# Polysketch attention and an exact-GELU MLP: keys of batches 1 to 3 by sketches as the stationary operand, numerators next to the query sketches

## The chip, the cores and the metric

The kernel runs on one core of one Trainium2 chip. The metric is the device time of one execution, in microseconds. The kernel before took 267.11 us, the median of three runs (266.31 to 267.64). Its profiled execution spans 264.9 us from the first to the last instruction, with a granted TensorE clock of 1.000.

## The reference

A polynomial-sketch attention (batch B = 4, H = 4 heads, S = 1088 tokens, head size D = 32, sketch size R = 8) feeds an MLP (128 to 2048 to 128, exact GELU) on 4352 tokens. Everything is float32 on the chip.

```python
def phi(x):                                   # 8 + 8 sketches, 64 features per token and head
    a = np.einsum('rd,bhsd->bhsr', S1, x)
    b = np.einsum('rd,bhsd->bhsr', S2, x)
    return np.einsum('bhsi,bhsj->bhsij', a, b).reshape(*x.shape[:-1], r * r)
q_p, k_p = (phi(q), phi(k))
kv = np.einsum('bhsf,bhsd->bhfd', k_p, v)     # sums over the tokens of a batch
z = np.sum(k_p, axis=2)
num = np.einsum('bhsf,bhfd->bhsd', q_p, kv)
den = np.einsum('bhsf,bhf->bhs', q_p, z)[..., None] + 1e-06
attn = num / den
...
h = x @ w_in                                  # x: attn as (B*S, H*D)
g = 0.5 * h * (1.0 + erf(h * inv_sqrt2))
return g @ w_out
```

Of a batch, 1024 tokens are handled in two chunks of 512; the last 64 tokens of all four batches make a ninth chunk of 256.

## The kernel before, in words

**Steps.** The MLP is the long part. A chunk n has 16 steps (fi = 0 to 15), one for each 128 columns of the hidden layer. In a step `hidden` (L691) lets TensorE make one hidden product of xT[n] and w_in into one of two PSUM tiles `h_ps` (bufs=2, L697, in two halves of 64 columns), and ScalarE applies the GELU (L704) into a `block` of four steps. Two steps later or more, `two_products` (L769) multiplies blocks with w_out (L782). It is a seven-product scheme in which GpSimd first adds halves of a block (`token_sums`, L739, four operations a block), and `drain` (L787) takes the two accumulators `o_ps` apart: three ScalarE copies (L794 to L796), six VectorE additions (L798 to L803). `combine` and `store` (L812, L835) finish a chunk and send it out. Chunks 0 and 1 are handled half in this way, half directly.

**Attention between the steps.** The rest is put in at fixed steps, by `at(t, f)` into `slots`. For chunk n, t = (n - 1) * 16 is the first step of chunk n - 1:

- `query_turn` at t - 6: VectorE turns the queries (L535).
- `query_sketch` at t: eight matmuls with S_abc[b] as the stationary operand in tiles of 64x32, 256 columns each (L584). S_abc[b] holds the sketches S1 and S2 and a factor that depends on the batch's z.
- `query_outer` at t: some fifteen VectorE operations turn the sketches in PSUM (L596), make the denominator and the outer products and turn these (L619).
- `attend` at t + 7: eight matmuls of features and kz[b], the numerators (L633, also 64x32 tiles of 256 columns), and a ScalarE copy into xT[n] (L637).

**Keys of batches 1 to 3.** `load_turned_k` brings the keys of a head in four transfers, so that `key_turn_blocks` can turn them 32x32-wise on VectorE (L353). `features_of_all` (at step 16 for batch 1, t + 6 for batch 2, t + 5 for batch 3) multiplies the turned keys kT, as the stationary operand in 64x64 tiles, with the sketches S12: 32 matmuls of 32 columns each (`key_products`, L368), and lets ScalarE copy half of the sketches from PSUM (L954). `outer_of_all` makes the features k_p in four VectorE products (L964), and `add_tokens` adds half and half over the tokens, down to a quarter for k_s (L413, L416; by GpSimd for batch 1, by VectorE else). `add_last` (L418) finishes k_s for batches 2 and 3 with the remainder tokens. `kv_sum` (L449, in `finish_keys`, at step 21 for batch 1, at t + 14 else) sums k_p with v on TensorE, and k_s with `ones` (L446), and `turn_kv` one step later turns the result into kz[b] and, over `sketch_of_z`, into S_abc[b].

**What sets the order.** Each engine works through its own queue. The kernel's last lines tie each instruction to the one before it on its engine, so that the order on an engine is the order of the text: in a step the drain comes first, then the hidden product and its GELU, the token sums, the slots, the store, the products of earlier blocks. PSUM is full: two banks `h_ps`, two `o_ps`, and four in two tiles `w_ps` that keys, sketches, numerators and kv sums take in turn.

Of the kernel before, what the change touches and what calls it, by code (L numbers as in the profile page):

```python
# [16 lines left out]
def kernel(  # L17
# [21 lines left out]
    F = R * R  # L39
# [27 lines left out]
    def work_banks():  # L67

        return wps.tile([128, 2, CW], FP, name="w_ps")
# [4 lines left out]
    def halves(banks):  # L74
        return [banks[:, i] for i in range(2)]
# [23 lines left out]
    def load_main(eng, n, b, heads=slice(0, H)):  # L99
        eng.dma_start(out=main[n, b][:, heads],  # L100
                      in_=src_of[n][b, heads, 0:MAIN, :].rearrange("h (p j) d -> p h j d", j=J))

    def load_turned_k(b):

        src = k[b, :, 0:MAIN, :].rearrange("h (jj t pb jc) d -> h pb t jj (jc d)", jj=4, t=32, pb=4)
        for h in range(H):
            for pb in range(4):
                sp.dma_start(out=main["k", b][pb * 32:(pb + 1) * 32, h].rearrange("t (jj jc) d -> t jj (jc d)", jj=4),
                             in_=src[h, pb])

    def load_q(n):
        at = n % NCH * CW
# [85 lines left out]
    def load_rest():  # L198

        load_w_out(1, gated=True)  # L200
        for i in range(2, len(pieces)):
            load_w_in(i)
            load_w_out(i)
        for b in range(1, B):
            load_turned_k(b)
            load_main(sp, "v", b)
# [19 lines left out]
    kz_first = big.tile([128, 128], FP, name="kz_first")  # L226

    ones = big.tile([128, D], FP, name="ones")

    ones_rem = big.tile([128, D], FP, name="ones_rem")  # L230
    pool.memset(ones_rem, 0.0)
    pool.memset(ones_rem[:REM], 1.0)
# [116 lines left out]
    def key_turn_blocks(b, r):  # L349

        kT[r] = att.tile([128, CW], FP, name="kT")
        for i in range(2):
            dve.transpose(out=kT[r][:, i * 256:(i + 1) * 256].rearrange("p (jc jj t) -> p jj jc t", jc=2, jj=4),  # L353
                          in_=main["k", b][:, r + 2 * i].rearrange("p (jj jc) d -> p jj jc d", jj=4))

    def spread(out, a, b):

        n = a.shape[1]
        return dict(out=out, in0=a[:, :, :, None].broadcast_to([128, n, R, R]),
                    in1=b[:, :, None, :].broadcast_to([128, n, R, R]))  # L360

    def key_products(r, banks, col=0):

        for i in range(2 * NCH):
            for c in range(2):
                for t in range(2):
                    at = i * 128 + c * 64
                    pe.matmul(banks[t][c * 64:(c + 1) * 64, col + i * 32:col + (i + 1) * 32],  # L368
                              lhsT=kT[r][t * 64:(t + 1) * 64, at:at + 64],
                              rhs=S12[t * 64:(t + 1) * 64, 2 * t:2 * t + 2].rearrange("p h r -> p (h r)"),  # L370
                              start=True, stop=True)
# [33 lines left out]

    k_s = {}

    def add_tokens(b, r, eng):

        words = mlp.tile([128, LC], U32, name="bits_r")  # L410
        k_s[r] = words.bitcast(FP).rearrange("p (c two one f) -> p c two one f", c=NP, two=2, one=2)
        kp = k_p[b, r].rearrange("p t (c two one) i j -> p t c two one (i j)", c=NP, two=2)
        eng.tensor_add(out=k_s[r].rearrange("p c two one f -> p (c two one f)"),  # L413
                       in0=kp[:, 0].rearrange("p c two one f -> p (c two one f)"),
                       in1=kp[:, 1].rearrange("p c two one f -> p (c two one f)"))
        eng.tensor_add(out=k_s[r][:, :, 0], in0=k_s[r][:, :, 0], in1=k_s[r][:, :, 1])  # L416

    def add_last(b, eng):  # L418

        rows = slice(b // 2 * REM, (b // 2 + 1) * REM)  # L420
        for r in range(2):
            to = k_s[r][:, :, 0, 0]
            eng.tensor_add(out=to, in0=to, in1=k_s[r][:, :, 0, 1])
            eng.tensor_add(out=to[rows], in0=to[rows], in1=k_p_rem[b % 2][rows, r::2].rearrange("p c i j -> p c (i j)"))

    def flat(features):
        return features.rearrange("p i j -> p (i j)")

# [15 lines left out]
    def kv_product(ps, lhsT, features, h, part, start=False, stop=False):  # L444

        pe.matmul(ps[h * D:(h + 1) * D, part * F:(part + 1) * F], lhsT=lhsT, rhs=features, start=start, stop=stop,  # L446
                  skip_group_check=True)

    def kv_sum(b, ps):  # L449


        for i in range(J):
            ch, t, one = i % 2, i // 4, i // 2 % 2
            for h in range(H):
                kv_product(ps, main["v", b][:, h, i, :], flat(k_p[b, h % 2][:, t, h // 2 * 4 + ch * 2 + one]), h, 0,
                           start=i == 0)
        for h in range(H):
            kv_product(ps, v_rem_aug[b][:, h, :], flat(k_p_rem[b % 2][:, h]), h, 0, stop=True)
        if b == 1:
            for h in range(H):  # L460
                kv_product(ps, ones_rem, flat(k_p_rem[b][:, h]), h, 1)
        for m in range(2 if b == 1 else 1):
            for h in range(H):
                kv_product(ps, ones, k_s[h % 2][:, h // 2, 0, m], h, 1, stop=b > 1 or m == 1)

    kv_T = {}

# [9 lines left out]
        sketch_of_z(b, banks[:, 0], F)  # L477


    S_abc = [big.tile([128, 2, 2, 2 * R], FP, name=f"S_abc{b}") for b in range(B)]  # L480
    own_r = big.tile([128, 2], FP, name="own_r")

    def spread_sketches():

        pool.tensor_add(out=own_r, in0=mask4[:, 0:2], in1=mask4[:, 2:4])
        own = own_r[:, None, :, None]
        w = S_abc[0]
        pool.memset(w, 0.0)
        pool.tensor_mul(out=w[:, :, :, 0:4], in0=sT[:, 0:R].rearrange("p (i f) -> p i f", i=2)[:, :, None].broadcast_to([128, 2, 2, 4]),
                        in1=own.broadcast_to([128, 2, 2, 4]))  # L490
        pool.tensor_mul(out=w[:, :, :, R:], in0=sT[:, None, None, R:].broadcast_to([128, 2, 2, R]),
                        in1=own.broadcast_to([128, 2, 2, R]))
        for b in range(1, B):
            pool.tensor_copy(out=S_abc[b], in_=w)

# [445 lines left out]


    def features_of_all(b):
        banks = halves(work_banks())
        for r in range(2):
            key_products(r, banks, r * 128)
        held["keys"] = banks


        held["factors"] = []  # L950
        for r in range(2):
            a = att.tile([128, 2, J, 2 * R], FP, name="a_t")
            for t in range(2):
                act.copy(out=a[:, t, :, 0:R], in_=factors(banks[t], r)[:, :, 0:R])  # L954
            held["factors"].append(a)

    def factors(bank, r):
        return bank[:, r * 128:(r + 1) * 128].rearrange("p (n r) -> p n r", r=2 * R)

    def outer_of_all(b, adds_by=dve):  # L960
        for r, a in enumerate(held["factors"]):
            k_p[b, r] = att.tile([128, 2, J, R, R], FP, name="k_p")
            for t in range(2):
                dve.tensor_mul(**spread(k_p[b, r][:, t], a[:, t, :, 0:R], factors(held["keys"][t], r)[:, :, R:2 * R]))  # L964
        for r in range(2):
            add_tokens(b, r, adds_by)

    held = {}

# [26 lines left out]
    round_at(14, w_out_sb[4], pool)  # L996
    at(15, query_turn, 2)
    at(16, features_of_all, 1)
    at(16, outer_of_all, 1, pool)
    at(16, turn_keys_rem, 1)  # L1000
    at(17, features_rem, 1)
    at(18, channel_sums, 4)

    at(21, finish_keys, 1)
    at(22, lambda: turn_kv(1, held["kv"]))
    at(23, query_turn, 3)
    at(23, query_sketch, 2)
    at(23, query_outer, 2)
    at(29, attend, 2)
    for i, t in enumerate((25, 26, 28)):  # L1010
        at(t, channel_sums, i)
    at(11, spread_sketches)
# [2 lines left out]
    for n in range(3, NCHUNK):  # L1015

        t = (n - 1) * NF
        b = (n + 1) // 2
        keys = n % 2 and b < B
        if n > 3:  # L1020
            at(t - 6, query_turn, n)
        at(t, query_sketch, n)
        at(t, query_outer, n)
        if keys:
            for r in range(2):
                at(t - 2, key_turn_blocks, b, r)

        at(t + 7, attend, n)
        if keys:
            at(t + 5 + (n == NCH + 1), features_of_all, b)  # L1030
            at(t + 5 + (n == NCH + 1), outer_of_all, b)
            at(t + 6, add_last, b, dve)
            at(t + 8, widen_v_rem, b)
            at(t + 14, finish_keys, b)
            at(t + 15, lambda b=b: turn_kv(b, held["kv"]))


    products = {t: [] for t in range(len(steps) + LAG)}
# [114 lines left out]
```

## Time and profile before

| Engine | busy us | share of the span | instructions |
|---|---|---|---|
| TensorE, matmuls | 258.7 | 98% | 2489 |
| TensorE, weight loads | 133.4 | 50% | 2489 |
| GpSimd | 170.2 | 64% | 180 |
| VectorE | 146.7 | 55% | 315 |
| ScalarE | 118.0 | 45% | 239 |

A float32 matmul stands as two records in the trace, and the end of a matmul is modelled, so that the distance from one start to the next says more than a duration. The costliest group by far is the hidden products (L697), 138.6 us; the products with w_out (L782) come in several groups by operand. The groups that the change touches are small: key products of batches 1 to 3 (L368 into `w_ps`) 3.4 us in 192 records, query sketches (L584) 4.0 and 0.5 us, numerators (L633) 4.0 and 0.7 us, the kv sums of batches 1 to 3 (L446) 5.5 us. On VectorE L964 takes 7.4 us, the additions over tokens (L413, L416, L423, L424) 13.3 us; on GpSimd L413 and L416 take 3.9 us.

The profile tells of each group how long the engine stood idle before it and what ended that. For an engine that isn't the bound such idle time costs nothing by itself; it matters where another engine waits for what comes after.

### The profile page before, as it was taken

The page shows a single profiled execution, that of the slowest core. Times are in us where ns is not written, and L with a number is a line of the kernel's source. Part 1 is how long each engine was busy: PE and PEld are TensorE (multiplying, and loading weights), DVE is VectorE, ACT ScalarE, POOL GpSimd, SP SyncE. Part 2 cuts the span into 40 slices and gives each one's busy share as a digit, 9 for nine tenths or more (in the row PEclk, how much of TensorE's full clock was granted, in tenths as well). Part 3 has the DMA queues.
Part 4 walks back from the last instruction along what each step waited for, and adds up shares of the span by engine and source line. Part 5 has one row for each costly group of instructions (what it writes and reads, how often), then busy time and mean ns, then how long its engine had stood idle before and what let it go on. Part 6 is the DMA issues. An engine that isn't in the chain of part 4 may idle for free.

```text
span 264.9 us, 6135 instructions
## 1 busy us (share of the span) xinstructions
PE 258.7 (98%) x2489; PEld 133.4 (50%) x2489; DVE 146.7 (55%) x315; ACT 118.0 (45%) x239; POOL 170.2 (64%) x180
## 2 busy tenths in 40 slices
PE   8999999999999999999999999999999999999995
PEld 6745445344444545444444554444444444445794
DVE  2985878455499995882086974670276015600240
ACT  5574767523634533353335333533345333533441
POOL 3613007899996876686767786686768677867300
PEclk9999999999999999999999999999999999999999
DMA  6479263433400201102000002002000200020021
GB/s 202 133 223 345 62 177 65 132 89 77 147 13 4 32 10 17 25 2 40 0 2 2 1 7 37 0 2 41 0 0 11 33 2 0 2 40 0 2 36 24
DMA packets 35755, 13.50 MB, mean 51 GB/s; under 512 B 28432, under 2 KB 34320, under 8 KB 35728
## 3 DMA queue, kind: packets, MB, share of 16 engines
q1 hardware_dynamic: 35536, 13.05, 19.5%
q8 instruction: 19, 0.31, 0.5%
q10 hardware_dynamic: 192, 0.07, 0.1%
q14 instruction: 8, 0.07, 0.1%
HBM read 10.88 MB, written 2.23 MB: 49 GB/s over the span
## 4 chain that ended last, share of the span: by engine, by line
PE 93%; DVE 2%; DMA 2%; ACT 1%; issue 1%; SPq 0%; POOL 0%; DVEq 0%
PE h_ps L697 43%; PE o_ps L782 33%; PE o_ps L833 5%; PE w_ps L830 3%; DMA q<-in_q_dram 2%; PE w_ps L584 2%; PE w_ps L633 1%; PE w_ps L446 1%; PE w_ps L368 1%; ACT block L704 1%; PE o_ps L435 0%; PE h_ps L712 0%; PE w_ps L550 0%; PE w_ps L649 0%; DVE x_tok L670 0%
## 5 line engine op out<-in xcount | busy, mean ns | idle before, releaser
L697 PE MATMUL h_ps<-xT,w_in 128*64 128x512 f32 (+3 forms) x516 | 138.6, 576 | 0.0
L704 ACT ACTIVATE block<-h_ps 128x512 f32<-128x512 f32 (+1 forms) x128 | 73.1, 571 | 120.3 <-PE h_ps L697 120.2
L782 PE MATMUL o_ps<-block,w_out 128*64 128x256 f32 x224 | 58.2, 382 | 0.0
L697 PEld LDWEIGHTS h_ps<-xT,w_in 128*64 128x64 f32 (+1 forms) x516 | 42.4, 143 | 28.8 <-issue 10.6
L747 POOL TENSOR_TENSOR bits_low<-block 128x512 f32<-128x512 f32 x28 | 36.0, 1286 | 25.5 <-ACT block L704 25.5
L782 PEld LDWEIGHTS o_ps<-block,w_out 128*64 128x64 f32 x224 | 29.4, 137 | 35.5 <-issue 24.2
L748 POOL TENSOR_TENSOR bits_a<-block 128x512 f32<-128x512 f32 x28 | 35.8, 1277 | 14.7 <-ACT block L704 14.7
L749 POOL TENSOR_TENSOR bits_e<-bits_a,block 128x512 f32<-128x512 f32 x28 | 36.3, 1297 | 2.2
L750 POOL TENSOR_TENSOR bits_m<-block,bits_e 128x512 f32<-128x512 f32 x28 | 36.0, 1284 | 2.2
L782 PE MATMUL o_ps<-bits_a,small 128*64 128x256 f32 x112 | 29.2, 383 | 0.0
L782 PE MATMUL o_ps<-bits_low,small 128*64 128x256 f32 x112 | 29.0, 382 | 0.0
L782 PE MATMUL o_ps<-bits_m,w_out 128*64 128x256 f32 x112 | 29.0, 382 | 0.0
L782 PE MATMUL o_ps<-block,small 128*64 128x256 f32 x112 | 29.0, 382 | 0.0
L596 DVE STREAM_TRANSPOSE w_ps<-w_ps 128x512 f32<-128x512 f32 (+1 forms) x7 | 4.8, 686 | 40.8 <-PE w_ps L584 40.7
L798 DVE TENSOR_TENSOR sums<-o_ps,sums 64x512 f32<-64x512 f32 x8 | 5.5, 683 | 37.6 <-ACT sums L795 26.4
L782 PEld LDWEIGHTS o_ps<-block,small 128*64 128x64 f32 x112 | 14.8, 137 | 19.8 <-issue 11.3
L782 PE MATMUL o_ps<-bits_e,small 128*64 128x256 f32 x112 | 16.8, 379 | 0.0
L833 PE MATMUL o_ps<-g,w_out 128*128 128x512 f32 x32 | 16.4, 599 | 0.1
L782 PEld LDWEIGHTS o_ps<-bits_m,w_out 128*64 128x64 f32 x112 | 14.8, 137 | 0.0
L782 PEld LDWEIGHTS o_ps<-bits_low,small 128*64 128x64 f32 x112 | 14.8, 137 | 0.0
L782 PEld LDWEIGHTS o_ps<-bits_a,small 128*64 128x64 f32 x112 | 14.6, 137 | 0.0
L782 PEld LDWEIGHTS o_ps<-bits_e,small 128*64 128x64 f32 x112 | 8.0, 137 | 11.0 <-issue 9.4
(186 smaller groups left out, 304.7 us busy)
## 6 DMA issues: line engine op xcount, KB each, us to landing
block<-in_moe_w_in_dram SPq DMA_DIRECT2D x3, 512.0 KB, 7.8
block<-in_moe_w_out_dram SPq DMA_DIRECT2D x3, 512.0 KB, 11.5
k<-in_k_dram SPq DMA_DIRECT2D x48, 32.0 KB, 1.8
v<-in_v_dram SPq DMA_DIRECT2D x3, 512.0 KB, 4.3
q<-in_q_dram SPq DMA_DIRECT2D x24, 64.0 KB, 3.4
out_dram<-oT SPq DMA_DIRECT2D x24, 64.0 KB, 2.2
k<-in_k_dram SPq DMA_DIRECT2D x2, 256.0 KB, 2.8
q<-in_q_dram SPq DMA_DIRECT2D x2, 256.0 KB, 4.1
```

The source lines that it names most:

```text
L584: pe.matmul(ps[q4 * 32:(q4 + 1) * 32, c, i * N:(i + 1) * N], lhsT=S_abc[batch_of(n, s, i)][rows, fh].rearrange("p r x -> p (r x)"), rhs=qT ...
L596: dve.transpose(out=tok, in_=ps[:, :, :H2])
L697: pe.matmul(ps[rows, :W], lhsT=w[:, rows], rhs=xT[n][:, :W], start=True, stop=True)
L704: act.activation(out=g_of[n, fi][:, :W], in_=ps[:, :W], func=ACT.Gelu)
L747: pool.tensor_sub(out=s[3], in0=a11, in1=a21)
L748: pool.tensor_add(out=s[1], in0=a21, in1=a22)
L749: pool.tensor_sub(out=s[2], in0=s[1], in1=a11)
L750: pool.tensor_sub(out=s[4], in0=a12, in1=s[2])
L782: pe.matmul(acc[n][bank][half * 64:(half + 1) * 64, col:col + HW], lhsT=fixed, rhs=moving, start=opens and e == 0 and name in "4715", stop ...
L798: dve.tensor_add(out=C[lo, 1], in0=a1[lo], in1=C[lo, 0])
L830: pe.matmul(o_of[n][i][:, :128], lhsT=g[:, i * 128:(i + 1) * 128], rhs=w_tile(w_out_sb, fi), start=first, stop=final)
L833: pe.matmul(o_of[n], lhsT=w_tile(w_out_sb, fi), rhs=g, start=first, stop=final)
```

## The change

Keys of batches 1 to 3 are now handled as the queries are. They are loaded by four transfers a batch, a quarter of the partitions for each head, and turned in two VectorE operations. The sketches S_ab become the stationary operand (eight matmuls of 64x32 tiles and 256 columns in place of 32 of 32 columns), the result is turned in PSUM, and the features come from two VectorE products of 1024 elements. The sum over tokens is then two reductions on VectorE, from k_p into PSUM, for all batches; of the 128 partitions of the sum one half is copied into k_s by ScalarE, the other gets the remainder tokens added by VectorE on the way. The values are loaded in the order that belongs to it. Fewer TensorE instructions, less work in additions and one way for all batches are what it is for.

Beside this, the numerators of chunk n - 1 and the sketches of chunk n now stand directly one after the other, one step before chunk n - 1 begins. They have the same tile shape.

```diff
-    def load_turned_k(b):
+    def load_keys(b):
...
         for h in range(H):
-            for pb in range(4):
-                sp.dma_start(out=main["k", b][pb * 32:(pb + 1) * 32, h].rearrange("t (jj jc) d -> t jj (jc d)", jj=4),
-                             in_=src[h, pb])
+            sp.dma_start(out=main["k", b][h * 32:(h + 1) * 32].rearrange("t x j d -> t (x j d)"),
+                         in_=k[b, h, 0:MAIN, :].rearrange("(t n) d -> t (n d)", t=32))
...
     def features_of_all(b):
-        banks = halves(work_banks())
-        for r in range(2):
-            key_products(r, banks, r * 128)
-        held["keys"] = banks
...
-                act.copy(out=a[:, t, :, 0:R], in_=factors(banks[t], r)[:, :, 0:R])
...
+        ps = work_banks()
+        for g in range(4):
+            for c in range(NP):
+                rows = slice(c * 64, (c + 1) * 64)
+                pe.matmul(ps[g * 32:(g + 1) * 32, c, :CW // 2], lhsT=S_ab[rows].rearrange("p r x -> p (r x)"),
+                          rhs=kT[g // 2][rows, g % 2 * 256:(g % 2 + 1) * 256], start=True, stop=True)
+        held["keys"] = ps
...
+    def outer_of_all(b):
...
+        dve.transpose(out=tok, in_=ps[:, :, :CW // 2])
...
+        dve.tensor_copy(out=a, in_=x[:, :, :, 0:R])
...
+            dve.tensor_mul(out=features.rearrange("p n r (i j) -> p (n r) i j", i=R),
+                           in0=a[:, c, :, :, None].broadcast_to([128, 2 * J, R, R]),
+                           in1=x[:, c, :, None, R:].broadcast_to([128, 2 * J, R, R]))
...
+    def add_tokens(b):
+
+        sums = held["keys"][:, :, :2 * F]
+        for c in range(NP):
+            dve.tensor_reduce(out=sums[:, c], in_=k_p[b][c].rearrange("p n r f -> p (r f) n"), axis=mybir.AxisListType.X,
+                              op=AX.add)
+        k_s[b] = att.tile([128, H, F], FP, name="k_s", bufs=1)
+        to = k_s[b].rearrange("p (c r) f -> p c (r f)", c=NP)
+        rows, rest = (slice(x * REM, (x + 1) * REM) for x in (b // 2, 1 - b // 2))
+        act.copy(out=to[rest], in_=sums[rest])
+        dve.tensor_add(out=to[rows], in0=sums[rows], in1=k_p_rem[b % 2][rows].rearrange("p (c r) i j -> p c (r i j)", c=NP))
...
     at(16, features_of_all, 1)
-    at(16, outer_of_all, 1, pool)
+    at(16, outer_of_all, 1)
     at(16, turn_keys_rem, 1)
     at(17, features_rem, 1)
+    at(17, add_tokens, 1)
...
-        at(t, query_sketch, n)
-        at(t, query_outer, n)
+        at(t - 1, attend, n - 1)
+        at(t - 1, query_sketch, n)
+        at(t - 1, query_outer, n)
...
-        at(t + 7, attend, n)
+        if n == NMAIN:
+            at(t + 15, attend, n)
         if keys:
             at(t + 5 + (n == NCH + 1), features_of_all, b)
             at(t + 5 + (n == NCH + 1), outer_of_all, b)
-            at(t + 6, add_last, b, dve)
+            at(t + 5 + (n == NCH + 1), add_tokens, b)
             at(t + 8, widen_v_rem, b)
-            at(t + 14, finish_keys, b)
-            at(t + 15, lambda b=b: turn_kv(b, held["kv"]))
+            at(t + 13, finish_keys, b)
+            at(t + 14, lambda b=b: turn_kv(b, held["kv"]))
```

Not shown: the values are loaded in four transfers a batch; `kv_sum` takes k_s[b] for all batches in four matmuls, and `ones_rem` and its matmuls for batch 1 are gone; S_ab is made by GpSimd in `spread_sketches`.

More of the change, by code (lines that the diff above doesn't have):

```diff
@@ L101, in load_main, with load_values @@
                       in_=src_of[n][b, heads, 0:MAIN, :].rearrange("h (p j) d -> p h j d", j=J))
-    def load_turned_k(b):
-        src = k[b, :, 0:MAIN, :].rearrange("h (jj t pb jc) d -> h pb t jj (jc d)", jj=4, t=32, pb=4)
+    def load_keys(b):
         for h in range(H):
-            for pb in range(4):
-                sp.dma_start(out=main["k", b][pb * 32:(pb + 1) * 32, h].rearrange("t (jj jc) d -> t jj (jc d)", jj=4),
-                             in_=src[h, pb])
+            sp.dma_start(out=main["k", b][h * 32:(h + 1) * 32].rearrange("t x j d -> t (x j d)"),
+                         in_=k[b, h, 0:MAIN, :].rearrange("(t n) d -> t (n d)", t=32))
+    def load_values(b):
+        src = v[b, :, 0:MAIN, :].rearrange("h (t q n) d -> q t h (n d)", t=32, q=4)
+        for g in range(4):
+            sp.dma_start(out=main["v", b][g * 32:(g + 1) * 32].rearrange("t h n d -> t h (n d)"), in_=src[g])
     def load_q(n):
@@ L204, in load_rest @@
         for b in range(1, B):
-            load_turned_k(b)
-            load_main(sp, "v", b)
+            load_keys(b)
+            load_values(b)
             for c in range(NCH):
@@ L228 @@
     ones = big.tile([128, D], FP, name="ones")
-    ones_rem = big.tile([128, D], FP, name="ones_rem")
-    pool.memset(ones_rem, 0.0)
-    pool.memset(ones_rem[:REM], 1.0)
     v_rem_aug = [big.tile([128, H, D if b else 2 * D], FP, name=f"v_rem_aug{b}") for b in range(B)]
@@ L347, in key_turn, with key_turn_blocks @@
         kT[r] = transposed(ps, "kT", [four_tokens("k", b, h, c) for h in (r, r + 2) for c in range(NCH)], copy, midway)
[L349 to L354, printed above, removed]
+    def key_turn_blocks(b, x):
+        kT[x] = att.tile([128, CW], FP, name="kT")
+        dve.transpose(out=kT[x], in_=main["k", b][:, 2 * x:2 * x + 2].rearrange("p x j d -> p (x j d)"))
     def spread(out, a, b):
@@ L406 @@
     k_s = {}
[L408 to L420, printed above, removed]
-        for r in range(2):
-            to = k_s[r][:, :, 0, 0]
-            eng.tensor_add(out=to, in0=to, in1=k_s[r][:, :, 0, 1])
-            eng.tensor_add(out=to[rows], in0=to[rows], in1=k_p_rem[b % 2][rows, r::2].rearrange("p c i j -> p c (i j)"))
     def flat(features):
@@ L452, in kv_sum @@
         for i in range(J):
-            ch, t, one = i % 2, i // 4, i // 2 % 2
             for h in range(H):
-                kv_product(ps, main["v", b][:, h, i, :], flat(k_p[b, h % 2][:, t, h // 2 * 4 + ch * 2 + one]), h, 0,
-                           start=i == 0)
+                kv_product(ps, main["v", b][:, h, i, :], k_p[b][h // 2][:, i, h % 2], h, 0, start=i == 0)
         for h in range(H):
             kv_product(ps, v_rem_aug[b][:, h, :], flat(k_p_rem[b % 2][:, h]), h, 0, stop=True)
[L459 to L464, printed above, removed]
+        for h in range(H):
+            kv_product(ps, ones, k_s[b][:, h], h, 1, stop=True)
     kv_T = {}
@@ L477, in turn_kv @@
         sketch_of_z(b, banks[:, 0], F)
+    S_ab = big.tile([128, 2, 2 * R], FP, name="S_ab")
     S_abc = [big.tile([128, 2, 2, 2 * R], FP, name=f"S_abc{b}") for b in range(B)]
@@ L492, in spread_sketches @@
                         in1=own.broadcast_to([128, 2, 2, R]))
+        pool.tensor_mul(out=S_ab, in0=sT[:, None].broadcast_to([128, 2, 2 * R]), in1=own_r[:, :, None].broadcast_to([128, 2, 2 * R]))
         for b in range(1, B):
@@ L943, in features_of_all @@
     def features_of_all(b):
-        banks = halves(work_banks())
-        for r in range(2):
-            key_products(r, banks, r * 128)
-        held["keys"] = banks
[L950 to L953, printed above, removed]
-                act.copy(out=a[:, t, :, 0:R], in_=factors(banks[t], r)[:, :, 0:R])
-            held["factors"].append(a)
-    def factors(bank, r):
-        return bank[:, r * 128:(r + 1) * 128].rearrange("p (n r) -> p n r", r=2 * R)
@@ L960, in outer_of_all @@
[L960 to L966, printed above, removed]
+        ps = work_banks()
+        for g in range(4):
+            for c in range(NP):
+                rows = slice(c * 64, (c + 1) * 64)
+                pe.matmul(ps[g * 32:(g + 1) * 32, c, :CW // 2], lhsT=S_ab[rows].rearrange("p r x -> p (r x)"),
+                          rhs=kT[g // 2][rows, g % 2 * 256:(g % 2 + 1) * 256], start=True, stop=True)
@@ new lines, in features_of_all @@
+        held["keys"] = ps
+    def outer_of_all(b):
+        ps = held["keys"]
+        tok = ps[:, :, CW // 2:]
+        dve.transpose(out=tok, in_=ps[:, :, :CW // 2])
+        x = tok.rearrange("p c (k x) -> p c k x", x=2 * R)
+        a = att.tile([128, NP, 2 * J, R], FP, name="a_t")
+        dve.tensor_copy(out=a, in_=x[:, :, :, 0:R])
+        k_p[b] = []
+        for c in range(NP):
+            features = att.tile([128, J, 2, F], FP, name="k_p")
+            dve.tensor_mul(out=features.rearrange("p n r (i j) -> p (n r) i j", i=R),
+                           in0=a[:, c, :, :, None].broadcast_to([128, 2 * J, R, R]),
+                           in1=x[:, c, :, None, R:].broadcast_to([128, 2 * J, R, R]))
+            k_p[b].append(features)
@@ new lines, in add_tokens @@
+    def add_tokens(b):
+        sums = held["keys"][:, :, :2 * F]
+        for c in range(NP):
+            dve.tensor_reduce(out=sums[:, c], in_=k_p[b][c].rearrange("p n r f -> p (r f) n"), axis=mybir.AxisListType.X,
[5 more added lines that the diff above has]
+        dve.tensor_add(out=to[rows], in0=sums[rows], in1=k_p_rem[b % 2][rows].rearrange("p (c r) i j -> p c (r i j)", c=NP))
@@ L1006 @@
     at(23, query_turn, 3)
-    at(23, query_sketch, 2)
-    at(23, query_outer, 2)
-    at(29, attend, 2)
+    at(24, query_sketch, 2)
+    at(24, query_outer, 2)
     for i, t in enumerate((25, 26, 28)):
```

## The prediction

> **What bounds the kernel now.** First the busy table and the chain of waits on the page:
>
> ```profile
> PE 258.7 (98%) x2489; PEld 133.4 (50%) x2489; DVE 146.7 (55%) x315; ACT 118.0 (45%) x239; POOL 170.2 (64%) x180
> ...
> PE 93%; DVE 2%; DMA 2%; ACT 1%; issue 1%; SPq 0%; POOL 0%; DVEq 0%
> ```
>
> TensorE is the bound: 98% busy and 93% of the chain. So a microsecond off its queue is a microsecond off the time, and so is a microsecond of waiting put into it. Second, who TensorE waits for after the start-up:
>
> ```profile
> PE w_ps L864 <- PEq L1137: 0.8, 1, 0.8
> PE w_ps L584 <- DVE S_abc L502: 0.7, 2, 0.6
> ```
>
> Only 0.7 us in two waits, both of a query sketch for its S_abc. Everything else arrives in time, and the question is how much in time. Third, TensorE's timeline at the keys of batch 3:
>
> ```profile
> 139.98 1.03 PE L697 MATMUL h_ps<-xT,w_in 128*64 128x512 f32 x4
> 140.94 1.14 PE L368 MATMUL w_ps<-S,kT 64*64 64x32 f32 x64
> 142.00 1.08 PE L697 MATMUL h_ps<-xT,w_in 128*64 128x512 f32 x4
> 142.91 0.38 PE L782 MATMUL o_ps<-block,small 128*64 128x256 f32 x1
> ...
> 144.21 1.03 PE L697 MATMUL h_ps<-xT,w_in 128*64 128x512 f32 x4
> 145.17 0.66 PE L633 MATMUL w_ps<-q_pT,kz 64*32 64x256 f32 x16
> 145.76 0.43 PE L782 MATMUL o_ps<-block,w_out 128*64 128x256 f32 x1
> ```
>
> Read the starts, since ends overlap. A hidden product (L697) takes 0.86 us, a pair of products (L782) 0.215. The key products take 1.06 plus 0.10 and 0.05 at their borders, 1.21 in all. The numerators (L633: 64x32 tiles, 256 columns) take 0.59 plus the same 0.15, so 0.74. Fourth, ScalarE at the drain before batch 2:
>
> ```profile
> 82.80 0.58 ACT L794 COPY sums<-o_ps 64x512 f32<-64x512 f32 x1
> 85.23 0.37 ACT L795 COPY sums<-o_ps 64x256 f32<-64x256 f32 x1 [1.85 <-DVE oT L845]
> 85.62 0.37 ACT L796 COPY sums<-o_ps 64x256 f32<-64x256 f32 x1
> 85.89 0.59 ACT L704 ACTIVATE block<-h_ps 128x512 f32<-128x512 f32 x1
> ```
>
> One copy waits 1.85 us for VectorE, and the GELU behind it runs only at 85.89 although its hidden product started at 82.72. That was hidden by the two h_ps buffers. Fifth, VectorE at batch 3, with the rows that price the new work:
>
> ```profile
> 141.05 0.68 DVE L798 TENSOR_TENSOR sums<-o_ps,sums 64x512 f32<-64x512 f32 x1 [1.84 <-PE h_ps L697]
> ...
> 143.62 0.42 DVE L803 TENSOR_TENSOR sums<-o_ps,sums 64x256 f32<-64x256 f32 x1
> 143.96 2.46 DVE L964 TENSOR_TENSOR k_p<-a_t,w_ps 128x512 f32<-128x512 f32 x4
> ```
>
> ```profile
> L616 DVE TENSOR_TENSOR q_f<-q_ac,w_ps 128x512 f32<-128x512 f32 x12 | 7.7, 684 | 0.2
> L413 DVE TENSOR_TENSOR bits_r<-k_p 128x512 f32<-128x512 f32 x4 | 5.4, 1343 | 0.0
> L596 DVE STREAM_TRANSPOSE w_ps<-w_ps 128x512 f32<-128x512 f32 x6 | 4.3, 723 | 26.6 <-PE w_ps L584 26.5
> L605 DVE TENSOR_REDUCE w_ps<-q_ac 128x32 f32<-128x128 f32 x6 | 1.8, 295 | 0.2
> ```
>
> **What the Trainium skill says.** "TensorE: Matmul & The Clock Gate", the table at its head: the queues of ScalarE and VectorE are strict FIFO. The trace agrees (the GELU at 85.89). The same page, "What's actually happening": TensorE falls to half clock after an idle window of about 3.4 us. The trace shows only the start: the first six matmuls (L864, 128x256) came 0.47 us apart, those of that size later 0.215. "Advanced Engine Details and Errata", "SBUF Cachelines": one access per 16-byte line costs a penalty, without a figure; no row here reads SBUF so. "SBUF — State Buffer", "Who interferes with whom": two SBUF inputs contend with GpSimd and a reduction doesn't; L413 with 1343 ns against L616 with 684 agrees on the first.
>
> **The change part by part.** *Keys.* 32 key products become 8 of the numerators' shape: 1.21 to 0.74 us, three times: -1.4. *Numerators next to sketches.* Six times two blocks of 0.74 become one with one set of borders and 0.43 us more (1024 cycles at the rate of L697): 1.17 instead of 1.48: -1.9. The hidden product that follows waits for xT: the GELU ahead (0.60) and the copy (0.59) end some 1.5 us after the last hidden product has been issued, and numerators, sketch and two products fill just that: 0. *Batch 1's kv sum* loses 16 of its records: -0.25. *Sketches after a batch change* now have products and a hidden product between turn_kv and themselves: the 0.7 us wait goes. *Loads, S_ab and GpSimd's lost additions* (3.9 us) lie beside TensorE: 0. Sum of what TensorE gains: -4.3.
>
> *The token sums.* Before, VectorE or GpSimd made all of k_s, and only the kv sum some eight steps later waited. Now act.copy in add_tokens moves one half of k_s, and stands in ScalarE's queue right behind the key step's GELU. It waits for VectorE: the drain, then transpose 0.73, copy 0.42 (as L679), two outer products of 1024 elements at 1.22 (L616's slope), two reductions of 1024. The reductions: L605 (128 elements, 295 ns) and L501 (64, 228 ns) give 1.05 ns an element, so 1.23 us; if the line penalty doubles the slope, 2.3. I take the middle, 1.75 each. Behind the copy stands the next GELU, which frees the h_ps buffer that the second hidden product after it needs, and TensorE runs in order. On the clock of before:
>
> - Batch 3: drain ends 144.04; transpose, copy and products to 147.75; reductions to 151.3; act.copy (0.37) to 151.7; GELU to 152.35; hidden product at 152.4. TensorE, from 139.98: hidden 0.96, sketches 0.6, hidden 0.9, three pairs of pairs 1.28, hidden 0.87, products 0.86: there at 145.45. It stalls 6.95.
> - Batch 2: VectorE has no idle time from the drain at 69.94 to that at 88.63, so TensorE gains nothing in there: it now arrives at the opening products at 85.6 and waits until 86.4 for L798 (+0.8, +0.1 for the second bank). Then 88.63 + 3.7 + 3.5 + 0.4 + 0.65 = 97.0 against 89.55: 7.4. Together 8.3.
> - Batch 1: no drain, but VectorE is rounding weights until 45.93. Then 3.65 for transpose to products, 0.41 for k_p_rem, 3.5 for the reductions, 0.45 and 0.65: GELU done at 54.75. TensorE has two more steps here and arrives at 49.82: 5.0.
>
> Sum of stalls +20.2. Stalls of 5 to 7 us may also cost the clock: at the page's window two or three of them would, each the half of some 2.8 us of slow running that the start shows, 1.4; I take 2.0 for all, between 0 and 4.2. Sum: 267.1 - 4.3 + 20.2 + 2.0 = **285.0**.
>
> **The rivals.** *TensorE's gain stands* (4%): if the copy doesn't hold the GELUs, 267.1 - 4.3 = 262.8, faster. For it: VectorE is idle 45% of the span. Against: it is busy just there (drain ahead, 3.65 us of outer products), and even with reductions for nothing batch 3's GELU would end at 148.9, 3.4 us late. *Short stalls* (6%): half the stalls hidden by an order or early readiness that I misread: 267.1 - 4.3 + 10 = 273. *Ends low* (20%): reductions at 1.23 and no clock loss: stalls 17.1, so 279.9. *Ends high* (20%): reductions at 2.3 and three cold starts: stalls 23.5 + 4.2, so 290.5. *VectorE as the bound throughout* speaks against itself: its sum falls, since L413, L416, L423 and L424 (13.3 us) give way to 6 reductions and small adds. The likeliest, 285.0, has 50%.
>
> **How the numbers follow.** From 279 to 291 takes in both ends of the reductions and of the clock, and leaves out the two rivals below (10%) and a little above. Faster by over 0.5%: 4% (the first rival). Within 0.5%: 1%, taken from the short stalls. Slower: 95%.
>
> **What would show it.** Right: ScalarE's longest waits are a 64x256 copy into k_s, for VectorE's reduction, three times, and TensorE has three gaps of 4 to 8 us at hidden products that wait for the GELU. Key sketches take about 0.6 us. The reduction's mean, near 1.2 or near 2.3 us, tells the penalty; matmuls at 0.43 us instead of 0.215 after a gap tell the clock. Wrong: gaps under 1 us there, or TensorE waiting for DMA or xT.

## The result and the profile after

| | before | after |
|---|---|---|
| time, median of 4 runs each, us | 267.16 (266.31 to 267.64) | 290.94 (290.1 to 292.11) |
| ratio to before, 95% interval | 1 | 1.0897 (1.0847 to 1.0947) |
| profiled span, us | 264.9 | 288.7 |
| mean granted TensorE clock | 1.000 | 0.963 |

The change costs 23.8 us. The forecast was 285.0, with 279 to 291 as the range. The direction and the mechanism were right; the time lies at the very end of the range, and one term of the sum, the slow clock, was far too small. The busy table and the chain of the page after, against those of before:

```profile
PE 264.1 (91%) x2329; PEld 133.8 (46%) x2329; DVE 150.7 (52%) x302; ACT 117.4 (41%) x230; POOL 165.4 (57%) x175
...
PE 68%; DVE 16%; SPq 6%; DMA 5%; ACT 2%; issue 1%; POOL 0%; DVEq 0%; ACTq 0%
```

TensorE runs 160 records fewer and is nevertheless busy 5.4 us longer, and its share of the chain falls from 93% to 68%; VectorE now holds 16% of it, against 2% before. Two things must have happened, waiting and slower matmuls. The waits of TensorE, then the longest wait of ScalarE on another engine's work (us in total, times, longest):

```profile
PE h_ps L673 <- ACT block L680: 18.4, 3, 7.2
PE o_ps L758 <- DVE sums L774: 1.0, 1, 1.0
```

```profile
ACT k_s L954 <- DVE w_ps L949: 24.7, 3, 9.5
```

Three waits of hidden products (L673) for the GELU (L680), and three waits of ScalarE's copy into k_s (L954) for VectorE's reduction (L949). How they belong together is read from the two timelines at the keys of batch 2, ScalarE's and then VectorE's:

```profile
91.09 0.59 ACT L680 ACTIVATE block<-h_ps 128x512 f32<-128x512 f32 x1
101.22 0.36 ACT L954 COPY k_s<-w_ps 64x256 f32<-64x256 f32 x1 [9.54 <-DVE w_ps L949]
101.49 1.07 ACT L680 ACTIVATE block<-h_ps 128x512 f32<-128x512 f32 x2
```

```profile
93.74 0.71 DVE L933 STREAM_TRANSPOSE w_ps<-w_ps 128x512 f32<-128x512 f32 x1
94.49 0.42 DVE L936 COPY a_t<-w_ps 128x256 f32<-128x256 f32 x1
94.95 2.35 DVE L940 TENSOR_TENSOR k_p<-a_t,w_ps 128x1024 f32<-128x1024 f32 x2
97.33 3.79 DVE L949 TENSOR_REDUCE w_ps<-k_p 128x128 f32<-128x1024 f32 x2
```

ScalarE finishes a GELU at 91.68 and does nothing until 101.22, because a copy of 0.36 us stands first in its queue and needs sums that VectorE completes at 101.12. Two GELUs follow the copy at once: their input had long been ready, since the later of the two hidden products that they read started at 92.91 (below). TensorE at the same place:

```profile
92.91 1.03 PE L673 MATMUL h_ps<-xT,w_in 128*64 128x512 f32 x4
...
94.57 0.38 PE L758 MATMUL o_ps<-block,w_out 128*64 128x256 f32 x1
94.58 0.38 PE L758 MATMUL o_ps<-bits_a,small 128*64 128x256 f32 x1
102.13 1.98 PE L673 MATMUL h_ps<-xT,w_in 128*64 128x512 f32 x4 [7.17 <-ACT block L680]
103.89 0.63 PE L758 MATMUL o_ps<-block,w_out 128*64 128x256 f32 x1
...
104.32 0.63 PE L758 MATMUL o_ps<-block,w_out 128*64 128x256 f32 x1
...
107.17 1.02 PE L673 MATMUL h_ps<-xT,w_in 128*64 128x512 f32 x4
108.02 0.38 PE L758 MATMUL o_ps<-block,w_out 128*64 128x256 f32 x1
```

The hidden product waits 7.17 us. But the rest of the loss stands in no column of waits. After the gap the hidden product takes 1.76 us (102.13 to 103.89) where that at 107.17 takes 0.85; pairs of products start 0.43 us apart (103.89, 104.32) where 0.215 is usual. One hidden product and two groups of four such pairs, 0.86 + 2 x 0.86 = 2.58 us of work, take from 102.13 to 107.17, 5.04 us. That is half speed for 5 us, and 2.46 us lost. The clock row of the page (granted clock in tenths, 40 slices) shows it as a 6 and an 8 for batch 1, a 5 for batch 2 and a 5 for batch 3:

```profile
PEclk9999999689999959999999959999999999999999
```

A slice is 7.2 us long, so such a stretch fills one slice or lies across two.

### The profile page after: what moved, and what is told of

It is laid out like the page before. It is cut to its first block, busy times and chain, and to the rows that moved or that the text cites. A ratio compares the mean times of both kernels' runs of the same rounds, so it can differ in the third digit from the quotient of the medians.

```text
span 288.7 us, 5753 instructions
## 1 busy us (share of the span) xinstructions
PE 264.1 (91%) x2329; PEld 133.8 (46%) x2329; DVE 150.7 (52%) x302; ACT 117.4 (41%) x230; POOL 165.4 (57%) x175
## 4 chain that ended last, share of the span: by engine, by line
PE 68%; DVE 16%; SPq 6%; DMA 5%; ACT 2%; issue 1%; POOL 0%; DVEq 0%; ACTq 0%
PE h_ps L673 32%; PE o_ps L758 27%; DVE w_ps L949 4%; DMA k<-in_k_dram 4%; PE w_ps L806 2%; DVE k_p L940 2%; SPq L121 2%; PE w_ps L426 1%; PE w_ps L609 1%; PE w_ps L840 1%; SPq L132 1%; SPq L106 1%; SPq L173 1%; PE w_ps L560 1%; DVE sums L776 1%
## 5 line engine op out<-in xcount | busy, mean ns | idle before, releaser
L673 PE MATMUL h_ps<-xT,w_in 128*64 128x512 f32 (+3 forms) x516 | 142.8, 593 | 18.4 <-ACT block L680 18.4
L680 ACT ACTIVATE block<-h_ps 128x512 f32<-128x512 f32 (+1 forms) x128 | 72.6, 570 | 119.8 <-PE h_ps L673 113.3
L673 PEld LDWEIGHTS h_ps<-xT,w_in 128*64 128x64 f32 (+1 forms) x516 | 42.6, 146 | 50.2 <-issue 17.6
L758 PE MATMUL o_ps<-block,w_out 128*64 128x256 f32 x224 | 59.6, 389 | 0.0
L758 PEld LDWEIGHTS o_ps<-block,w_out 128*64 128x64 f32 x224 | 30.9, 140 | 40.5 <-issue 27.6
L758 PE MATMUL o_ps<-block,small 128*64 128x256 f32 x112 | 29.9, 390 | 1.0 <-DVE sums L774 1.0
L758 PE MATMUL o_ps<-bits_m,w_out 128*64 128x256 f32 x112 | 30.5, 397 | 0.0
L758 PE MATMUL o_ps<-bits_low,small 128*64 128x256 f32 x112 | 29.9, 390 | 0.0
L774 DVE TENSOR_TENSOR sums<-o_ps,sums 64x512 f32<-64x512 f32 x8 | 5.5, 683 | 41.7 <-ACT sums L771 24.0
L758 PEld LDWEIGHTS o_ps<-bits_m,w_out 128*64 128x64 f32 x112 | 16.1, 144 | 0.0
L475 DVE TENSOR_TENSOR z_s<-w_ps,sT 128x64 f32<-128x64 f32 x4 | 0.9, 222 | 27.9 <-ACT kz L450 19.1
```

Source lines behind the costliest of these rows:

```text
L673: pe.matmul(ps[rows, :W], lhsT=w[:, rows], rhs=xT[n][:, :W], start=True, stop=True)
L680: act.activation(out=g_of[n, fi][:, :W], in_=ps[:, :W], func=ACT.Gelu)
L758: pe.matmul(acc[n][bank][half * 64:(half + 1) * 64, col:col + HW], lhsT=fixed, rhs=moving, start=opens and e == 0 and name in "4715", stop ...
```

## The experiments

The theory: (1) the copy's place in ScalarE's queue makes the three gaps, (2) the gaps make TensorE run slowly for a while after each. The rivals: the moved numerators make the next hidden product wait for xT; VectorE's new work is simply too long; the slow matmuls are something other than a consequence of idleness.

### The copy by another engine, or later

`copy_by_dve`:

```diff
-        act.copy(out=to[rest], in_=sums[rest])
+        dve.tensor_copy(out=to[rest], in_=sums[rest])
```

> The changed kernel with one word different: VectorE, not ScalarE, copies the half of the token sums into k_s. Theory (the copy in ScalarE's queue holds the GELUs): the three gaps of 4.7, 7.3 and 6.9 us at hidden products go, and with them the slow matmuls after each (some 7 us), so 291 - 19 - 7 = 265; batch 1's kv sum may then wait 1 to 2 us for k_s itself, so 265 to 267. Rival (VectorE's own work, above all the reductions, is what TensorE waits for): VectorE gets 0.4 us more per batch, so the time stays at 285 or more.

`copy_later` leaves the copy with ScalarE, but behind the GELUs of the steps between:

```diff
-        act.copy(out=to[rest], in_=sums[rest])
+        held['rest'] = lambda: act.copy(out=to[rest], in_=sums[rest])
...
+    at(20, lambda: held['rest']())
...
+            at(t + 12, lambda: held['rest']())
```

> The changed kernel with ScalarE's copy into k_s moved from the key step to step 20 (batch 1) or seven and six steps later (batches 2 and 3), when the reductions are done. No work changes, only the place in ScalarE's queue. Theory (place in the queue): 265 to 266.5, without gaps over 1 us for batches 2 and 3. Rival (the copy or the reductions cost by themselves): no change from 291.

Measured: 266.66 us, ratio 1.0002 (0.9986 to 1.0017), and 267.08 us, ratio 1.0005 (0.9993 to 1.0017). All of the loss is gone in both (copy_later lies 0.6 us above the range expected for it), with the same transposes, products and reductions on VectorE. The waits of TensorE in copy_by_dve, those over half a microsecond after the start-up:

```profile
PE w_ps L426 <- DVE k_s L955: 1.6, 1, 1.6
PE o_ps L758 <- DVE sums L774: 1.0, 1, 1.0
```

No hidden product waits for a GELU any more. So neither the length of VectorE's chain nor the copy's own 0.36 us is the cause, but the queue in which the copy waits. What is new is a wait of 1.6 us of batch 1's kv sum for k_s: there VectorE's chain does reach the path that sets the end.

### The numerators

`numerators_back` is the kernel after with numerators and query sketches where they stood before (core of the edit):

```diff
-        at(t - 1, attend, n - 1)
-        at(t - 1, query_sketch, n)
-        at(t - 1, query_outer, n)
+        at(t, query_sketch, n)
+        at(t, query_outer, n)
...
+        at(t + 7, attend, n)
```

> The changed kernel with numerators and query sketches at their places of before; keys stay new, ScalarE's copy too. Theory: the three gaps stay, so 291 to 292. Rival (numerators one step before their chunk make xT late): most of the 24 us go, 270 or less.

Measured: 289.7 us, ratio 1.0865 (1.0829 to 1.09). The three gaps stay (17.7 us of waiting for L680 instead of 18.4), so the rival with xT falls. The time is 1.3 us under the range expected; what that is worth is seen below.

`numerators_alone` is the reverse edit on the kernel before: only the numerators are moved.

> The kernel before with only the move: numerators of chunk n - 1 next to the sketches of chunk n. By the prediction six pairs at 0.31 us and the wait for S_abc: 264.6. If the border of 0.10 + 0.05 us belongs to a wait for VectorE and not to the tile shape, it comes back at the products that wait for the drain: 0.15 less for each pair, 265.5. Rival (xT late): over 267.5.

Measured: 267.12 us, ratio 0.9994 (0.9978 to 1.001). The gain that was expected is absent. The waits of TensorE name what took its place:

```profile
PE o_ps L782 <- POOL bits_e L749: 1.3, 1, 1.3
...
PE o_ps L782 <- DVE sums L798: 0.6, 1, 0.6
```

With the numerators gone from the middle of a chunk, products reach their GpSimd operand 1.3 us too early once, and an opening product waits 0.6 us for the drain.

### Keys alone

`keys_alone` is copy_by_dve with the numerators back: the key part of the change without its blocking copy.

> The kernel after with the copy into k_s given to VectorE, and with numerators and query sketches where they stood before: the key part of the change alone, without the copy that blocks. What the two parts are worth apart: the keys -1.4 and the kv sum -0.25, against one wait of 1.6 us for batch 1's k_s as in copy_by_dve. Theory (the moved numerators cost 1.2 us here, as 290.9 against 289.7 showed): 266.66 - 1.2 = 265.5. Rival (the moved numerators gain what the prediction said, 1.9, and only the stalls hid it): 266.66 + 1.9 + 0.7 = 269.3.

`keys_alone_kv_later` also gives VectorE one step more for batch 1's k_s:

```diff
-    at(21, finish_keys, 1)
-    at(22, lambda: turn_kv(1, held["kv"]))
+    at(22, finish_keys, 1)
+    at(23, lambda: turn_kv(1, held["kv"]))
...
-    at(23, query_sketch, 2)
-    at(23, query_outer, 2)
+    at(24, query_sketch, 2)
+    at(24, query_outer, 2)
```

> As keys_alone, with batch 1's kv sum, the turn of it and the sketches of chunk 2 one step later each, so that VectorE has 1.6 us more to finish k_s. If the wait of 1.6 us for k_s is what keeps keys_alone from its gain: 1.6 less than keys_alone, about 264. If the wait only passes to the sketches of chunk 2, which need S_abc of the same chain: the same as keys_alone.

Measured: 267.81 us, ratio 1.0023 (1.0009 to 1.0036), between the two values expected and near neither; and 266.48 us, ratio 0.9976 (0.9964 to 0.9988). Where keys_alone stands against before is seen by comparing the starts of the same hidden products in both traces (minus is earlier than before). They shift by -0.4 us up to and with batch 1's key step, +1.55 at its kv sum (the wait for k_s), 0 at batch 2's key step and -0.47 at batch 3's: +0.7 in all. Batch 2's key step saves nothing because the products behind it wait for the drain anyway, as the prediction said. The step later takes the k_s wait from 1.6 to 0.7 us and that for S_abc from 0.7 to 0.2; 1.4 us off the waits, 1.33 us off the time.

So the numerators' move is worth nothing measurable on the kernel before, -1.15 on the keys without blocking (267.81 to 266.66, with 22 executions each; 0.8 by their means), and +1.2 by the medians on the kernel after (289.7 to 290.94). The last isn't clear of noise: four executions each, 289.28 to 292.12 against 290.1 to 292.11. My expectation for keys_alone took it as a property of the move; it wasn't one. In numerators_back a block of numerators lies just ahead of batch 3's gap, which is 0.74 us shorter (6.35 instead of 7.09): they cost nothing where TensorE waits anyway. And its granted clock was 0.970 instead of 0.963: behind batch 1's gap half the clock was granted for 3.41 us, in after for 6.83.

### Is the slow running a matter of idleness?

`kept_warm` puts matmuls of zeros into the gaps of the kernel after (for batch 1 into a second PSUM bank that it takes with that of the remainder keys), and changes nothing else:

```diff
+    at(19, lambda: keep_busy(10, held['spare']))
...
+            at(t + 7 + (n == NCH + 1), lambda: keep_busy(15, work_bank()))
```

> The kernel after with dummy matmuls of zeros put into the three gaps of TensorE, 10 (4.3 us) for batch 1 and 15 (6.5 us) each for batches 2 and 3, into a free tile of PSUM. Nothing else changes, and the hidden products still wait for the same GELUs. Theory (the 7.0 us of half-rate matmuls after the gaps come from TensorE's idleness): they go, 290.9 - 7.0 = 283.9, the stalls of the GELU chain stay where they were and matmuls after them start 0.215 us apart. Rival (the slow stretch after a gap is not the clock but ScalarE catching up with the GELUs): unchanged, 290.9.

Measured: 284.28 us, ratio 1.0649 (1.0613 to 1.0684), 6.7 us less than after. TensorE at batch 2 (L840 are the zeros):

```profile
92.59 1.03 PE L673 MATMUL h_ps<-xT,w_in 128*64 128x512 f32 x4
93.55 6.80 PE L840 MATMUL w_ps<-const-float32-0.0 128*128 128x256 f32 x30
...
101.83 1.08 PE L673 MATMUL h_ps<-xT,w_in 128*64 128x512 f32 x4 [0.47 <-ACT block L680]
102.74 0.38 PE L758 MATMUL o_ps<-block,w_out 128*64 128x256 f32 x1
...
102.96 0.38 PE L758 MATMUL o_ps<-block,w_out 128*64 128x256 f32 x1
```

From the hidden product before the gap to the one behind it are 9.24 us (92.59 to 101.83), in the kernel after 9.22 (92.91 to 102.13), so the hold-up by the GELU is the same. But products behind it start 0.22 us apart. The slow stretch comes from TensorE's idleness, and 6.7 us is its price here. The same hidden products compared in both traces give 2.2 us for batch 1's gap, 2.4 for batch 2's and 2.1 for batch 3's.

### How long a gap has to be

`half_copy` lets ScalarE copy only the first head pair, after the first reduction, so each gap is about one reduction shorter:

```diff
...
-        act.copy(out=to[rest], in_=sums[rest])
+            if c == 0:
+                act.copy(out=to[rest, 0], in_=sums[rest, 0])
+        dve.tensor_copy(out=to[rest, 1], in_=sums[rest, 1])
```

> The kernel after with ScalarE copying only the first head pair of the sum, after the first of the two reductions, and VectorE the other pair. Each gap gets one reduction (1.88 us) shorter: about 2.8, 5.4 and 5.0 us, 14 us of stalls in place of 19.7. What happens to the slow stretch behind them tells what sets it. If any gap of some length brings one slow stretch of fixed length: the gaps of batches 2 and 3 still lose 2.1 to 2.45 us, and the one of 2.8 us either the same (285.3) or nothing (282.9). If the loss grows with the gap, by 7.0 / 19.7 = 0.36 us for each us: 290.9 - 5.6 - 2.0 = 283.3, with 1.0 us after the gap of 2.8.

`partly_warm` is kept_warm with 4 and 8 dummy matmuls in place of 10 and 15.

> As kept_warm with only 4 dummy matmuls for batch 1 and 8 each for batches 2 and 3, so that TensorE still stands idle in the gaps, for about 3.0, 3.7 and 3.4 us. Gaps of 4.7 us and more were followed by a slow stretch, one of 2.7 us was not; this looks between. If the slow clock needs more than 3.7 us of idleness: no slow stretch, 284. If it needs less than 3.0: all three, some 7 us in all, 290.5. Between: 2.1 to 2.4 us for each gap that brings one, 286 or 288.5.

Measured: 282.33 us, ratio 1.0567 (1.0537 to 1.0596), and 288.69 us, ratio 1.0811 (1.0765 to 1.0856). The same place in both, batch 1's gap, half_copy first:

```profile
52.43 1.94 PE L673 MATMUL h_ps<-xT,w_in 128*64 128x512 f32 x8 [2.54 <-ACT block L680]
54.30 1.10 PE L426 MATMUL w_ps<-k_p,v 128*32 128x64 f32 x64
55.21 0.29 PE L426 MATMUL w_ps<-k_p_rem,v_rem_aug 128*32 128x64 f32 x8
```

```profile
54.69 2.43 PE L673 MATMUL h_ps<-xT,w_in 128*64 128x512 f32 x8 [2.62 <-ACT block L680]
57.05 1.93 PE L426 MATMUL w_ps<-k_p,v 128*32 128x64 f32 x64
58.76 0.44 PE L426 MATMUL w_ps<-k_p_rem,v_rem_aug 128*32 128x64 f32 x8
```

The waits are alike, 2.54 and 2.62 us. In half_copy the kv sum's first 64 records then take 0.91 us, in partly_warm 1.71. In sum_in_a_row, below, a wait of 3.25 us at this place was followed by no slow matmuls either. So the length of a gap alone doesn't decide. In partly_warm the other two gaps (3.54 and 2.92 us of wait) were also followed by slow matmuls, and its four executions took 287.0, 287.4, 289.95 and 290.0 us at clocks of 0.986, 0.987, 0.976 and 0.976: the same program paid differently.

The Trainium skill, "TensorE: Matmul & The Clock Gate", "What's actually happening", says that the window in which activity is watched is free-running, so that the point of change depends on where in the window the work falls. The traces agree, and show the windows. In each of them the granted clock changes only at whole multiples of 3.413 us after it first rose to full: in after it rose at 4.61 us and changed at 52.40, 59.23, 100.19, 107.01, 165.04 and 171.87, which is 14, 16, 28, 30, 47 and 49 multiples later.

The span cut at these times, around batch 1's gap in half_copy, sum_in_a_row and partly_warm (stretch; its length; busy time of TensorE, its weight loads, VectorE, ScalarE and GpSimd; then the granted clock):

```profile
48.43:51.84 3.41, 1.46 (x8) 0.29 (x4) 3.08 (x4) 0.41 (x2) 0.16 (x1) 1.00 0.91 213
51.84:55.25 3.41, 2.82 (x76) 1.53 (x80) 2.54 (x3) 2.51 (x5) 2.81 (x3) 1.00 0.30 75
```

```profile
48.60:52.01 3.41, 1.50 (x8) 0.29 (x4) 3.38 (x4) 0.00 (x0) 0.20 (x1) 1.00 1.00 240
52.01:55.43 3.42, 2.08 (x24) 0.79 (x28) 0.59 (x2) 2.42 (x6) 2.15 (x2) 1.00 0.55 152
```

```profile
52.59:56.00 3.41, 1.31 (x6) 0.57 (x8) 1.35 (x2) 1.64 (x4) 1.37 (x2) 1.00 0.21 53
56.00:59.41 3.41, 3.41 (x86) 2.19 (x83) 0.00 (x0) 1.48 (x3) 3.25 (x3) 0.50 0.10 14
```

The first two gaps lie across two windows, with at most 1.95 and 1.91 us of idleness in one of them. Most of partly_warm's lies in one window, with 2.1 us of idleness, and the next window has half the clock. All thirteen traces follow this: the 26 windows at full clock with 2.1 us of idleness or more (13 of them at the programs' ends) were each followed by half the clock, and none with 1.95 or less was. The full clock came back after the first window in which TensorE was busy throughout, so that half the clock lasted one window (3.41 us, three times) or two (6.83 us, ten times). This is read from the traces, with idle times that rest on modelled ends of matmuls; no run moved a gap against the windows on purpose. The page asks for an idle window of some 3.4 us; here 2.1 us of idleness inside one was enough.

half_copy closes the sum. Of the three times expected (285.3, 282.9, 283.3) the one without a loss behind batch 1's gap is nearest, and the loss behind the other two doesn't shrink with the gap. The gaps are 3 x 2.0 us shorter, batch 1's slow stretch is gone (hidden products and kv sum to 55.21 take 2.78 us here and 5.01 in after, so it was worth 2.2), batch 2's lost 2.0 (in after 2.46) and batch 3's 2.9 (in after 2.1). -6.05 - 2.2 - 0.5 + 0.8 = -7.95, and the spans differ by 8.2. The expectations put 7.0 us on the three slow stretches, 0.2 too much on batch 1, because they counted its two hidden products at 1.72 us; undisturbed they take 1.87 there.

### The reduction's stride

`sum_in_a_row` adds eight neighbours instead of eight values 512 bytes apart, so its sums are of other elements than the reference's:

```diff
-in_=k_p[b][c].rearrange("p n r f -> p (r f) n")
+in_=k_p[b][c].rearrange("p n r f -> p (n r f)").rearrange("p (x n) -> p x n", n=J)
```

> The kernel after with its reductions reading k_p in the order in which it lies in memory, eight neighbours into one sum, instead of eight values 512 bytes apart. The sums are therefore of other elements than the reference's. It prices the stride. If the stride is what makes a reduction of 1024 elements 1.88 us: 1.23 each, at the slope of the short rows of before (1.05 ns an element), two in each of three chains, so stalls 3.9 us shorter and 287.0. If a reduction of 1024 elements costs 1.88 us in any order: unchanged, 290.9.

Measured: 287.07 us, ratio 1.0755 (1.0728 to 1.0783). The reductions, in the kernel after and here (busy us, mean ns of one):

```profile
L949 DVE TENSOR_REDUCE w_ps<-k_p 128x128 f32<-128x1024 f32 x6 | 11.3, 1879 | 0.2
```

```profile
L949 DVE TENSOR_REDUCE w_ps<-k_p 128x128 f32<-128x1024 f32 x6 | 7.4, 1227 | 0.2
```

Elements 512 bytes apart cost 1.83 ns each, neighbours 1.20. Each of the three gaps is 1.3 us shorter, and the median time 3.9 shorter. The slope from short rows had given 1.23 us for 1024 neighbours. The forecast of 287.0 took the clock's loss as unchanged; in the profiled execution, the shortest of five, it is 0.9 us smaller (none, 2.9 and 3.0 behind the three gaps), so that the exact hit owes something to luck.

### The best version

`both_kv_later` is copy_by_dve with batch 1's kv sum two steps later (one step more than in keys_alone_kv_later), and the sketches of chunk 2 one step later.

> A version meant to be the best: keys and numerators as in the kernel after, the copy into k_s by VectorE, and batch 1's kv sum, its turn two steps later and the sketches of chunk 2 one step later. The wait of 1.6 us for k_s in copy_by_dve should go and the rest stay: 266.66 - 1.6 = 265.1. Rival: VectorE, which works without a pause from there to batch 2's first drain, hands the delay on to that drain, where TensorE waits 1.0 us already: 266.7.

Measured: 265.14 us, ratio 0.9941 (0.9918 to 0.9964). The wait for k_s is gone from TensorE's list, the 1.0 us for the drain (L774) is still there and has not grown. This version is faster than both kernels, by 0.6% and by 8.9%.

## Why the prediction was right in kind and short in size

The sum as the prediction made it, and as the trace of after shows it:

| term | predicted | measured | from |
|---|---|---|---|
| stalls, batch 1 | 5.0 | 4.7 | gap of 5.14 between starts, less 0.43 |
| stalls, batch 2 | 8.3 | 8.1 | 0.75 at the opening products, 7.33 |
| stalls, batch 3 | 6.95 | 6.9 | gap of 7.09, less 0.21 |
| slow clock after them | 2.0 | 6.8 | 2.2 + 2.46 + 2.1 |
| TensorE's gain | -4.3 | -2.7 | what is left of 23.8 |

- **What bounds, and the copy in ScalarE's queue: right.** The stalls came out at 19.7 against 20.2, and both copy experiments removed them whole. The strict order of ScalarE's queue, taken from the Trainium skill ("TensorE: Matmul & The Clock Gate", the table at its head) and from one GELU of before, carried the forecast; the wait of 9.54 us at the copy, with two ready GELUs behind it, agrees. The working's chains are rounded up a little: 144.04 + 0.73 + 0.42 + 2.44 is 147.63, not 147.75, and batch 1's terms end at 54.59, not 54.75; the three stalls lose 0.4 us by it.
- **The clock: the step that failed.** I took 1.4 us per cold start from the six matmuls at the start of the program, "I take 2.0 for all, between 0 and 4.2". Each of the three gaps lost 2.1 to 2.46 us, and kept_warm gives 6.7 for all. Two errors: the slow running after a gap lasted 4.2 to 5 us (twice what it lost, at half rate), not the 2.8 us that the start-up shows (in before matmuls begin at 0.77 us and the full clock at 3.60), and I counted on only some of three gaps of 5 to 7 us being hit. In the trace half the clock stands for 6.83 us at each gap; it begins while TensorE still waits, and what is left of it falls on the work. Even the upper end, 4.2, was short. With 6.8 in place of 2.0 the sum is 289.8.
- **The reduction: mid-way guess, 1.88 against 1.75.** Both bounds (1.23 and 2.3) held, and sum_in_a_row shows that the lower one is the price without the stride. The error of 0.13, twice in each chain, was balanced by other parts of the chain: the stalls are not longer than forecast.
- **TensorE's gain: too large by 1.6.** Key sketches fell as predicted, from 1.06 to 0.59. The pairs did not gain 0.31 each. I had counted the 0.10 and 0.05 us beside a block of numerators as the price of a change of tile shape, saved when two blocks become one. They aren't only that: at copy_by_dve's middle of a chunk, with no numerators between, they are there as well:

```profile
116.03 1.03 PE L673 MATMUL h_ps<-xT,w_in 128*64 128x512 f32 x4
116.99 0.43 PE L758 MATMUL o_ps<-block,w_out 128*64 128x256 f32 x1
...
117.91 1.03 PE L673 MATMUL h_ps<-xT,w_in 128*64 128x512 f32 x4
```

  Starts are 0.96 and 0.92 us apart where 0.86 and 0.86 are usual. A pair takes 0.46 + 0.57 = 1.03 instead of 2 x 0.59, so it saves 0.15, and six save 0.9 instead of 1.9. What makes these 0.10 and 0.06 us, no run here tells. Of the rest, 0.2 is a wait for xT at the last chunk; some 0.4 I can't place.
- **Rivals.** "The gain stands" and "short stalls" fell with the waits. "Ends high", 290.5, has nearly the measured time, but by other terms: it needed reductions of 2.3 us, which took 1.88, and only 4.2 us for the clock.

## What to carry to other kernels

A small instruction put on an idle engine isn't free if its input is late: all that stands behind it in that engine's queue waits too, so ask whose input it needs and what is queued behind it, and place it where its input is already there. Price a gap in TensorE as the gap plus the slow matmuls behind it, here 1.7 to 3.0 us lost each time. Whether they come depends on how the gap lies in the clock's windows of 3.41 us. An estimate from the 1.95 and 2.1 us above: a gap of over 4.2 us brings them wherever it lies, one under 1.9 us alone doesn't, and one between may in one execution and not in the next. Look for them in distances between starts, since no wait column shows them. What a rearrangement is worth must be weighed with the waits of the same kernel: the same move of the numerators was worth nothing on one, -1.15 us on the next, and nothing clear of noise on the third.

## What the runs showed of the hardware that I had not expected

- The granted clock changed only at multiples of 3.413 us in all thirteen traces. A window of that length with 2.1 us of idleness or more was followed by half the clock, one with 1.95 or less wasn't, and the full clock came back after a window that was busy throughout.
- After the ten waits of 4.5 to 7.2 us in after, numerators_back, half_copy and sum_in_a_row TensorE ran at half rate for 3.4 to 6.0 us, and lost 1.7 to 3.0 us each time. Waits of 2.54 and 3.25 us were followed by none; those of 2.62, 2.92 and 3.54 us in partly_warm by 3.4, 3.4 and 5.6 us of it.
- In partly_warm the slow running did not begin with the first matmul after batch 1's gap: two hidden products from 54.69 on took 2.36 us instead of 1.87 as in half_copy, so they lost 0.49, while the kv sum behind them ran at about half speed (1.71 instead of 0.91). The clock fell at 56.00, after the work had come back.
- A reduction on VectorE over elements 512 bytes apart costs 1.5 times that over neighbours (1879 against 1227 ns for 1024 elements a partition).
